# Gated linear attention with a SiLU block: state products per head in halves of the array's columns, first states copied by ScalarE, and a flag's product placed later

## Chip, cores and metric

The kernel runs on one core of one Trainium2 chip, in one launch. The metric is the device time in microseconds (us), the median of three runs. Beside it there is one profiled execution, with a record of every instruction of every engine.

## The reference

Batch 4, 8 heads, 768 steps, head dimension 48. Per head a state of 48x48 is decayed by `alpha`, row by row, and gets the outer product of `k` and `v` added; the output is `q` times the state. The result, as 3072 rows of 384, goes through a block `silu(x @ w_in) @ w_out` with 2048 hidden columns.

```python
for t in range(S):
    state = alpha[:, :, t, :, None] * state + np.einsum('bhd,bhe->bhde', k[:, :, t], v[:, :, t])
    y[:, :, t] = np.einsum('bhd,bhde->bhe', q[:, :, t], state)
...
x = y.transpose(0, 2, 1, 3).reshape(B * S, H * D)
h = x @ w_in
out = (h / (1 + np.exp(-h))) @ w_out
```

## The kernel before

**Chunks.** Time is cut into 6 chunks of 128 steps for each of the 4 batches: 24 chunks, numbered `n = 4 * ci + b`, so that chunks 0 to 3 are the first of each batch. Two heads stand side by side in a pair, head `u` of the pair in rows or columns `64 * u` to `64 * u + 47` of a 128-wide tile (16 are padding); there are `NP = 4` pairs. Each chunk goes through these functions:

- `products` (L652): transposes of alpha, k and q (by TensorE, L669, for the first eight chunks; by VectorE, L650, for the later ones), running products of alpha along time by scans (L674, L699), and k and q scaled by them. For the first chunks a copy on ScalarE (L671) brings alpha from PSUM.
- `scores` (L706): k times q for each head, in the two halves of the array's rows (L715), the causal mask on VectorE (L719), k transposed back (L723) and copied by ScalarE to `kn` (L725), and the decay of the state on ScalarE (L729).
- `values` (L734): the masked scores times v, and the state times q, in four quarters of 32 columns of the array (L749); ScalarE copies the result to `xt` (L754).
- `states` (L755): k times v over the 128 steps, into the state `st` of that batch. It is done for all but the last chunk of a batch, so 20 times.

In `states`, one matmul for a pair has `kn` of both heads as weights (128 columns) and `v` of both heads as moving data (64 + 48 = 112 columns). This computes four blocks; the two on the diagonal, k of a head with v of the same head, are read. VectorE adds them to `st` in two instructions of 48 rows by 192 (L768), or, in the first chunk of a batch, copies them there (L770).

All matmuls are in float32, and each one stands in the trace as two MATMUL and two LDWEIGHTS instructions.

**The block behind it.** `pieces` (L1037) is a list of slices of the second block's work: products with `w_in` (`enter_plain`, L805; `enter`, L828) and with `w_out` (`leave`, L926). Both use fewer matmuls than the plain product: sums of blocks of weights and inputs are formed on VectorE first, as in Strassen's method. One call of `go_on` (L1059) writes the next slice. After each of the four stages of a step, `fill` (L1083) writes as many slices as are due. `convert` brings the weights, which come as 64-bit numbers, to float32 (L599 on ScalarE, L602 to L604 on VectorE) during the first steps.

**Audits and the flag.** The shortcuts hold for bounded inputs. `audit` (L611) loads alpha and the weights once more, a part at a time into one buffer (L631), and VectorE keeps their extremes (L639). At the end four checks (L1138, L1139) are combined to `good` (L1141), one small matmul sums it over the partitions (L1143), VectorE turns that into `small` (L1144), and all engines load it as a number. If it is 0, a second, general version of the whole kernel runs (it does not for these inputs). Around this, the last slices of the second block are written:

```python
ps = ps_attn()[0:1, 0, 0:1]
pe.matmul(ps, lhsT=good, rhs=mask[:, C - 1 : C], start=True, stop=True)
dve.tensor_single_scalar(small, ps, 127.5, ALU.is_ge)
for _ in range(6):
    go_on()
```

**What sets the order.** The program text is not the order of the engines' queues. The framework puts the instructions of each engine into an order of its own, from dependences and its own estimates; `keep_in_program_order` pins a few. Waits are set by data and by buffers. PSUM: three banks `ps_a` in turn for the attention stages and the flag, three `ps_m` for `enter`, two `ps_o` for `leave`. Loads and stores are issued by SyncE (SP).

Of the kernel before, what the change touches and what calls it, by code (L numbers as in the profile page):

```python
# [355 lines left out]
def quotients(  # L356
# [20 lines left out]
    pe, dve, act, gps = nc.tensor, nc.vector, nc.scalar, nc.gpsimd  # L377
    B, H, S, D = q.shape
# [39 lines left out]
    def ps_attn(n=C):  # L418
        return ps_a.tile([128, 512], F32, name="ps_a").rearrange("p (j c) -> p j c", c=n)
# [98 lines left out]
    st = [fix.tile([128, NP, 2, D], F32, name=f"st{b}") for b in range(B)]  # L518
# [236 lines left out]
    def states(n):  # L755
        c = ctxs.pop(n)
        ci, b, vn = c["ci"], c["b"], c["v"]
        if ci < NCH - 1:
            ps = ps_attn(64)
            vn = vn.rearrange("p (j u) d -> p j (u d)", u=2)[:, :, 0 : 64 + D]  # L760
            for j in range(NP):
                pe.matmul(ps[:, 2 * j : 2 * j + 2, :].rearrange("p u d -> p (u d)")[:, 0 : 64 + D],
                          lhsT=c["kn"][:, j, :], rhs=vn[:, j], start=True, stop=True)
            for u in range(2):
                r = slice(64 * u, 64 * u + D)
                s, x = st[b][r, :, u, :], ps[r, u::2, 0:D]
                if ci > 0:
                    dve.tensor_tensor(s, x, s, ALU.add)  # L768
                else:
                    dve.tensor_copy(s, x)  # L770

    def block_x(grp, at):

# [285 lines left out]
    def go_on():  # L1059

        nonlocal done
        next(pieces[done][0], None)
        done += 1
# [36 lines left out]
    for step in range(STEPS):  # L1100
        stages = [[(scores, 1)], [(products, 0)], [(values, 1)], [(states, 1)]]
        if step < GB:

            stages = stages[1::-1] + stages[2:]
        elif step >= NA:
            stages = [[(scores, 1)], [(products, 0)], [(values, 1), (states, 1)], [(quotient, 0)]]
        for slot, group in enumerate(stages):
            for stage, lag in group:
                n = step - lag
                if not 0 <= n < NT:  # L1110
                    continue
                stage(n)
                if stage is values:
                    bridged = n + 1
                if stage is products and n + NIN < NA:
                    load(n + NIN)
                if stage is quotient and n + 1 < NT:
                    load(n + 1)
                if stage is states and n + NV < NT:
                    load_v(n + NV)  # L1120
            fill(step, slot)
            if step >= NA - 1 and slot > 0 and conv_done[1] == NFT and not late:
                settle()
# [15 lines left out]
        dve.tensor_single_scalar(e, e, bound, holds)  # L1139
    good = work.tile([128, 1], F32, name="good")  # L1140
    dve.tensor_reduce(good, ends, axis=AX, op=ALU.min)  # L1141
    ps = ps_attn()[0:1, 0, 0:1]
    pe.matmul(ps, lhsT=good, rhs=mask[:, C - 1 : C], start=True, stop=True)  # L1143
    dve.tensor_single_scalar(small, ps, 127.5, ALU.is_ge)  # L1144
    for _ in range(6):
        go_on()
    within = nc.values_load(small[0:1, 0:1], min_val=0, max_val=1)
    traced = nc.cur_bb.bb.instructions
# [8 lines left out]
@with_exitstack  # L1157
def kernel(
    ctx: ExitStack,
    tc: tile.TileContext,  # L1160
    q: bass.AP,
    k: bass.AP,
    v: bass.AP,
    alpha: bass.AP,
    moe_w_in: bass.AP,
    moe_w_out: bass.AP,
    out: bass.AP,
):


    flag = ctx.enter_context(tc.tile_pool(name="flag", bufs=1))
    small = flag.tile([1, 1], I32, name="small")
    args = (q, k, v, alpha, moe_w_in, moe_w_out, out)
    within = quotients(tc, small, *args)
    with tc.If(within < 1, label="general"):
        general(tc, *args)
# [30 lines left out]
```

## Time and profile before

| | |
|---|---|
| three runs | 583.13, 583.20 and 584.03 us, median 583.2 |
| span of the profiled execution | 582.0 us |
| granted clock of TensorE | 0.998 |
| busy: PE, PEld | 564.4 us, 500.4 us |
| busy: DVE, ACT, POOL | 452.6 us, 185.5 us, 7.3 us |
| state products (L762) | 160 MATMUL, 160 LDWEIGHTS |
| adds to the states (L768), copies (L770) | 32 of 350 ns, 8 of 354 ns |

PE is TensorE multiplying and PEld TensorE loading weights, DVE is VectorE, ACT ScalarE, POOL GpSimd, SP SyncE. In a line of a group stand the source line, the engine, the operation, output and inputs by name, the part of the array in use (rows*columns), the shape of the moving data and the count, and then busy us and the mean duration in ns. The ends of matmuls are modelled, so distances between starts say more on TensorE than durations. "Idle before" is the time for which the engine stood still ahead of these instructions, and who released it.

### The profile page before, as it was taken

What the parts mean: (1) busy time and instruction counts of PE and PEld (TensorE: products, weight loads), DVE (VectorE), ACT (ScalarE), POOL (GpSimd) and SP (SyncE); (2) the same over time, 40 slices, a digit from 0 to 9 for tenths busy, and PEclk for the clock granted to TensorE, in tenths of its full rate; (3) what the DMA queues carried; (4) which work ended last, traced back from release to release, by engine and by line L of the source; (5) the groups of instructions that cost most, each with busy time, mean ns of one, the idle gap of its engine ahead of it and who ended that gap; (6) DMA issues with size and microseconds to landing.
All of it is one profiled execution on the core that took longest, in us unless ns stands there. A gap on an engine that the chain in (4) does not pass through costs nothing. (4 is left out here: it accounts for less than half of the span.)

```text
span 582.0 us, 10743 instructions
## 1 busy us (share of the span) xinstructions
PE 564.4 (97%) x4290; PEld 500.4 (86%) x4290; DVE 452.6 (78%) x815; ACT 185.5 (32%) x359; POOL 7.3 (1%) x25
## 2 busy tenths in 40 slices
PE   5899999999999999999999999999999999999986
PEld 4777887678999899899899899899899999998986
DVE  5788899899788699996997886897872875766751
ACT  2235443222312233442433433342332342322100
POOL 5000000000000000000000000000000000000000
PEclk9999999999999999999999999999999999999999
DMA  9997885444534314442414433423110113424320
GB/s 211 174 276 195 218 210 131 88 111 117 128 89 125 112 33 124 123 115 71 119 48 120 122 74 86 129 53 105 57 44 22 51 44 115 123 88 129 96 72 30
DMA packets 93898, 63.70 MB, mean 109 GB/s; under 512 B 54800, under 2 KB 85520, under 8 KB 93840
## 3 DMA queue, kind: packets, MB, share of 16 engines
q1 hardware_dynamic: 93840, 62.94, 42.8%
q8 instruction: 35, 0.57, 0.4%
q14 instruction: 23, 0.19, 0.1%
HBM read 58.20 MB, written 4.72 MB: 108 GB/s over the span
## 5 line engine op out<-in xcount | busy, mean ns | idle before, releaser
L926 PE MATMUL ps_o<-w_out,g 128*128 128x192 f32 x704 | 122.3, 327 | 1.3 <-DVE o L940 1.1
L926 PEld LDWEIGHTS ps_o<-w_out,g 128*128 128x128 f32 x704 | 115.2, 190 | 4.2 <-DVE o L940 1.9
L926 PE MATMUL ps_o<-wt,g 128*128 128x192 f32 x528 | 91.6, 326 | 0.5 <-DVE u L1002 0.5
L805 PE MATMUL ps_m<-xt,w_in 128*128 128x256 f32 x384 | 88.9, 382 | 1.2 <-DVE w_in L604 1.1
L926 PEld LDWEIGHTS ps_o<-wt,g 128*128 128x128 f32 x528 | 87.2, 190 | 2.2 <-DVE u L1002 0.8
L805 PEld LDWEIGHTS ps_m<-xt,w_in 128*128 128x128 f32 x384 | 70.7, 190 | 11.0 <-DVE w_in L604 2.3
L828 PE MATMUL ps_m<-xc,w_in 128*128 128x256 f32 x288 | 70.0, 379 | 0.0
L639 DVE TENSOR_REDUCE seen<-bits 128x1 f32<-128x384 int32 (+2 forms) x65 | 42.4, 688 | 27.6 <-DMA bits<-in_moe_w_out_dram 21.2
L828 PEld LDWEIGHTS ps_m<-xc,w_in 128*128 128x128 f32 x288 | 54.1, 190 | 6.2
L834 ACT COPY g<-ps_m 128x512 f32<-128x512 f32 x64 | 37.1, 586 | 41.9 <-PE ps_m L828 41.9
L828 PE MATMUL ps_m<-xc,wx 128*128 128x256 f32 x192 | 49.8, 382 | 0.0
L931 DVE TENSOR_TENSOR g<-g 128x512 f32<-128x512 f32 x66 | 44.6, 686 | 4.8 <-PE ps_o L926 4.7
L839 ACT ACTIVATE g<-g 128x1024 f32<-128x1024 f32 x32 | 33.2, 1056 | 44.0 <-DVE g L842 44.0
L729 ACT ACTIVATE st<-st,u 128x96 f32<-128x96 f32 x80 | 25.7, 368 | 51.9 <-DVE u L674 36.8
L842 DVE TENSOR_TENSOR g<-ps_m,g 128x512 f32<-128x512 f32 x56 | 37.6, 684 | 2.9 <-PE ps_m L828 2.7
L828 PEld LDWEIGHTS ps_m<-xc,wx 128*128 128x128 f32 x192 | 35.0, 190 | 3.9 <-issue 0.4
L719 DVE TENSOR_TENSOR g<-ps_a,mask 128x512 f32<-128x512 f32 x48 | 31.2, 684 | 7.6 <-PE ps_a L715 7.3
L674 DVE TENSOR_TENSOR_SCAN u<-al,one 128x516 f32<-128x516 f32 x24 | 29.2, 1221 | 6.4 <-ACT al L671 6.4
L699 DVE TENSOR_TENSOR_SCAN p<-al,inv 128x516 f32<-128x516 f32 x24 | 29.5, 1228 | 4.8 <-PE ps_a L749 4.2
L834 ACT COPY part<-ps_m 128x512 f32<-128x512 f32 x32 | 18.8, 587 | 42.4 <-PE ps_m L828 38.1
L808 ACT ACTIVATE g<-ps_m 128x512 f32<-128x512 f32 x32 | 19.0, 594 | 41.6 <-PE ps_m L805 41.6
L715 PEld LDWEIGHTS ps_a<-p,u 48*128 48x128 f32 x384 | 24.6, 193 | 8.4 <-issue 6.7
(117 smaller groups left out, 657.3 us busy)
## 6 DMA issues: line engine op xcount, KB each, us to landing
bits<-in_moe_w_in_dram SPq DMA_DIRECT2D x24, 512.0 KB, 3.9
bits<-in_moe_w_out_dram SPq DMA_DIRECT2D x32, 384.0 KB, 3.4
at<-in_alpha_dram SPq DMA_DIRECT2D x64, 96.0 KB, 2.3
kt<-in_k_dram SPq DMA_DIRECT2D x64, 96.0 KB, 2.7
qt<-in_q_dram SPq DMA_DIRECT2D x64, 96.0 KB, 2.4
vn<-in_v_dram SPq DMA_DIRECT2D x24, 192.0 KB, 3.2
bits<-in_alpha_dram SPq DMA_DIRECT2D x9, 512.0 KB, 3.8
out_dram<-o SPq DMA_DIRECT2D x48, 96.0 KB, 1.8
```

The lines of the kernel that those rows point to most:

```text
L639: dve.tensor_reduce(seen[kind][which][:, i : i + 1], x, axis=AX, op=op, apply_absolute_value=True))
L674: dve.tensor_tensor_scan(u[:, end - 1 :: -1], sg[:, end:0:-1], one[:, end:0:-1], 0.0, ALU.mult, ALU.add)
L699: dve.tensor_tensor_scan(p[:, 0:end], sg[:, 0:end], iv[:, 0:end], 0.0, ALU.mult, ALU.add)
L719: dve.tensor_tensor(g[:, u], ps[u], mask[:, None, :].to_broadcast([128, NP, C]), ALU.mult)
L729: act.mul(s[:, j], s[:, j], c["all"][:, j : j + 1])
L805: pe.matmul(ps[:, e, :], lhsT=w_in[:, t, (f + e) * 128 : (f + e + 1) * 128], rhs=xt[:, t, :], start=(t == 0), stop=(t == NKT - 1))
L828: pe.matmul(ps[:, e], lhsT=block_w(w)[:, 2 * pair + e], rhs=block_x(grp, x), start=(first and e == 0), stop=(e == 1), skip_group_check=True)
L834: act.copy(to, ps)
L839: act.activation(x, x, AF.Silu)
L842: dve.tensor_tensor(to, a, b, op)
L926: pe.matmul(ps, lhsT=x, rhs=w[:, i], start=(first and i == 0), stop=(i == HF - 1), skip_group_check=True)
L931: dve.tensor_tensor(cells(grp, h, pair, *to), cells(grp, h, pair, *x), cells(grp, h, pair, *y), ALU.subtract)
```

## The change

There are three parts.

1. In `states`, a matmul takes one head: 48 weight columns and 48 moving columns, with its output in the 64 PSUM partitions that belong to its half of the array's columns. There are eight of them for a chunk in place of four, the two heads of a pair one after the other, all in one `ps_a` bank.
2. In the first chunk of a batch, ScalarE copies the result to `st` in place of VectorE.
3. Two slices of the second block are written ahead of the flag's product, and four after it in place of six.

```diff
         if ci < NCH - 1:
-            ps = ps_attn(64)
-            vn = vn.rearrange("p (j u) d -> p j (u d)", u=2)[:, :, 0 : 64 + D]
+
+            ps = ps_attn()
             for j in range(NP):
-                pe.matmul(ps[:, 2 * j : 2 * j + 2, :].rearrange("p u d -> p (u d)")[:, 0 : 64 + D],
-                          lhsT=c["kn"][:, j, :], rhs=vn[:, j], start=True, stop=True)
+                for u in range(2):
+                    r = slice(64 * u, 64 * u + D)
+                    pe.matmul(ps[r, j, 0:D], lhsT=c["kn"][:, j, r], rhs=vn[:, 2 * j + u, 0:D],
+                              start=True, stop=True)
             for u in range(2):
                 r = slice(64 * u, 64 * u + D)
-                s, x = st[b][r, :, u, :], ps[r, u::2, 0:D]
+                s, x = st[b][r, :, u, :], ps[r, :, 0:D]
                 if ci > 0:
                     dve.tensor_tensor(s, x, s, ALU.add)
                 else:
-                    dve.tensor_copy(s, x)
+                    act.copy(s, x)
...
     dve.tensor_reduce(good, ends, axis=AX, op=ALU.min)
+    go_on()
+    go_on()
     ps = ps_attn()[0:1, 0, 0:1]
     pe.matmul(ps, lhsT=good, rhs=mask[:, C - 1 : C], start=True, stop=True)
     dve.tensor_single_scalar(small, ps, 127.5, ALU.is_ge)
-    for _ in range(6):
+    for _ in range(4):
         go_on()
```

In the program after the change the lines behind `states` stand two further on, and those behind the flag's product four.

## The prediction, made before the changed kernel was run

> **What bounds the kernel now.** I read the share of each engine first, then the busy time by stretch, the waits of TensorE, the groups by shape, and last the timeline of TensorE around one state product.
>
> The first two lines are from the page (engines over the span), the others from the table by stretch (start:end, width, then busy us of PE, PEld, DVE, ACT, POOL).
>
> ```profile
> PE 564.4 (97%) x4290; PEld 500.4 (86%) x4290; DVE 452.6 (78%) x815; ACT 185.5 (32%) x359; POOL 7.3 (1%) x25
> 60.00:400.00 340.00, 340.00 (x2769) 299.84 (x2768) 293.68 (x521) 117.69 (x243) 0.00 (x0) 1.00 0.43 111
> 480.00:560.00 80.00, 77.81 (x432) 72.92 (x430) 50.89 (x100) 19.42 (x31) 0.00 (x0) 1.00 0.38 113
> ```
>
> From 60 to 480 us TensorE is busy all the time, and asked for its waits between 60 and 400 the trace names none. So in that stretch time is TensorE's own work and nothing else; DVE has 46 us of 340 free. It waits for others only at both ends:
>
> ```profile
> PE ps_o L669 <- DVE p L704: 1.4, 1, 1.4
> PE ps_m L805 <- DVE w_in L604: 1.1, 1, 1.1
> PE ps_o L669 <- DVE u L681: 0.7, 1, 0.7
> ...
> PE ps_a L1143 <- DVE good L1141: 1.5, 1, 1.5
> ```
>
> The first three are of the first 60 us, where DVE (weights being converted, scans) holds TensorE; the last is the flag's product, for which TensorE stands at 559.6 to 561.1. It ends a chain of audits, each a load of 3 to 4 us and then its reductions on DVE, that is linked load by load from about 482 us on. Before that the loads are long there when DVE comes to them, so the start of that chain moves with TensorE.
>
> What the state products cost, by shape (us, mean ns) and in order of time (start us, us):
>
> ```profile
> L762 PE MATMUL ps_a<-vn,kn 128*128 128x112 f32 x160 | 24.3, 293 | 0.0
> L762 PEld LDWEIGHTS ps_a<-vn,kn 128*128 128x128 f32 x160 | 20.6, 198 | 4.3 <-issue 3.6 <-ACT kn L725 0.2 <-DVE w_out L603 0.2
> L770 DVE COPY st<-ps_a 48x192 f32<-48x192 f32 x8 | 2.8, 354 | 2.4 <-PE ps_a L762 2.3
> ...
> 311.81 1.08 PE L749 MATMUL ps_a<-g,vn 128*32 128x128 f32 x32
> 312.71 0.84 PE L749 MATMUL ps_a<-p,st 128*32 128x128 f32 x24
> 313.48 1.15 PE L762 MATMUL ps_a<-vn,kn 128*128 128x112 f32 x8
> 314.46 0.61 PE L828 MATMUL ps_m<-xc,wx 128*128 128x256 f32 x2
> ```
>
> Durations of PE are modelled, so I go by starts. Each product is two MATMUL instructions (160 for 20 chunks of 4). The eight of a chunk begin at 313.48 and the next group at 314.46: 0.98 us, of which eight steps of 0.112 are 0.89 and 0.09 is the first weight load that nothing hides. In narrow stretches of the timeline the last four L749 start at 313.26, which is 0.22 before L762, though rounds of four are 0.11 apart ((312.71 - 311.81)/8). So a whole block, from the last four tiles of the values to the next full-array matmul, is 1.18 us; it is 1.18 in all 15 chunks from the sixth on.
>
> **What the Trainium skill says.** "TensorEngine Tiling (Array Packing)", Key Properties: tiles of the array load and multiply independently, a 128-row array can be split into two tiles of 64 columns, and changing the tiling mode drains the engine. The trace agrees where it can: 32 values in 0.90 us are 28 ns each, while 192 columns take 162 ns (16 of L926 in 2.60 us, so 0.85 ns a column): four tiles must run side by side. No run here shows halves of 64 columns. "TensorE: Matmul & The Clock Gate", LDWEIGHTS: a load costs its columns over 1.2 GHz, whatever the rows. The trace agrees: the eight loads of 128 columns start 0.112 apart (107 by that price), which is longer than 112 moving columns need (112 x 0.85 = 95). So the state products are bound by weight loads, half of which are for cross products that nobody reads. The same page gives small matmuls a floor of about 25 ns from start to start; in the trace four tiles start within 20 ns, so it isn't one for tiles.
>
> **The change part by part.**
>
> *State products.* Out go 8 instructions of 128 weight columns and 112 moving ones for each of 20 chunks; in come 16 of 48 and 48. If the halves run side by side as the quarters do, that is 8 rounds. One round is the longer of the load, estimated by the skill's price as 48/1.2 = 40 plus the 5 that the trace adds (112 against 107), and 48 moving columns (48 x 0.85 = 41): 45 ns. Around them stand two changes of mode where there was one. In: 0.20 from the last tile to the first state product (as 313.28 to 313.48 now), plus a first load of 48 columns in the open, about 0.04 (for 32 columns the second round of L749 comes 0.025 late, for 128 it is 0.10). Out: the drain, 0.09 (0.20 less the round of 0.11), and the next full load in the open, 0.10, against 0.015 that is lost there now: 0.09 net. The out case without states stands in the trace at 401.79, where the second L828 comes 0.32 after the first instead of 0.215. Block: 0.20 + 0.04 + 8 x 0.045 + 0.09 + 0.09 = 0.78 us, against 1.18: 0.40 saved, 15 times: 6.0 us. Chunk 4 stands between full-array matmuls (L805 on both sides, block 1.09 now), so it gets both changes new: 0.31 + 0.04 + 0.36 + 0.18 = 0.89, 0.2 saved. Bounds for a round: 41 (load alone) gives 0.43 saved, 60 ns gives 0.28; so 4.3 to 6.7 for the 16 chunks. The sums of L768 keep their shape (48x192) and are fewer cycles later only.
>
> *The first 60 us* (chunks 0 to 3 and the copies). Chunk 0's block runs at the slow clock, 2.33 us from tile to tile; by the same sum with its loads at about 82 ns it is 1.2, so 1.1 less, and the chain values, copy of xt (L754), `up` (L599), w_in (L604), scan (L674) follows it. The eight copies leave DVE (2.8 us, and 2.3 of waiting that DVE did in its order for L762). They go to ACT, 25% to 35% busy there: a copy of 128x192 on ACT is 0.31 us (L938), so 0.6 a chunk, in front of L754, which waits 1.5 us longer for the values anyway in chunk 0. Behind them in ACT's order stand `up` and the al copy; the weight conversion waits for those, so up to 0.6 us a chunk can come back. The built order of the changed kernel is another one up to chunk 3 (states and values split differently, one piece of scores put ahead of twelve L805, and those scores now wait on ACT for a ps_a bank), and from chunk 4 on the same on TensorE. TensorE's waits of 20 to 60 us are 3.0 us in all, and its work falls by 1.1 and about 0.9; so I bound the gain by 4 and by 0, and take 2.0.
>
> *The flag's product.* In the source it stands two pieces later. In the built order nothing moves: on TensorE it comes after the same 8 L926 as before with the same 6 + 8 + 8 + 16 + 8 behind it, and DVE, ACT and SP have the same order there too. 0, and the 1.5 us of standing stays. POOL's order is the same. In SP's queue some loads of a chunk change places among themselves; DVE waits for such loads 2.3 us in the whole span now (the transposes of kt), so I take 0, between -0.5 and 0.5.
>
> Sum: 6.0 + 0.2 + 2.0 + 0 = 8.2 us. Own span 582.0 gives 573.8; the timed runs of before have a median of 583.2, so I take the same off: 575.0. The saving reaches the end since the audits' chain starts when DVE, paced by TensorE, gets to it.
>
> **Rivals.**
> First, the halves run one after another with loads hidden: 16 turns of 45 ns, block 0.42 + 0.72 = 1.14, so 0.04 saved a chunk; chunk 4 loses 0.15. What is left is the start: 583.2 - 0.5 - 1.5 = 581.2. For it: no 64-column tile in this trace. Against: tiles of 32 columns and the pairs of 48 rows (L715) overlap.
> Second, slower: neither halves overlap nor loads hide in this mode. A turn is 41 + 43 = 84 ns, 16 of them 1.34; block 0.42 + 1.34 = 1.76, +0.58 in 15 chunks, and 0.75 more in chunk 4: about 583.2 + 9 = 592. It decides from 48 ns a turn for 16 serial turns ((1.18 - 0.42)/16), or 95 ns for 8 rounds. Against it: L749 starts its next loads as soon as its tiles multiply.
> Third, the start gets worse: ACT's copies in front of the al copy and `up` delay DVE by 0.6 us in each of four chunks and the new order loses a mode change or two (0.3 each). Then 6.2 - 3 = 3.2: 580.0.
> That the flag's part doesn't do what it says I hold for settled by the order.
>
> **How the numbers follow.** Side by side with a start between 0 and 4: 0.84; serial but hidden 0.06; slower 0.04; worse start 0.06. A measurement of this kernel tells about 0.2% (1.2 us) from no change. The likeliest case spans 583.2 - 4.3 = 578.9 to 583.2 - 10.7 = 572.5, taken as 572.4, and I reach to 579.2 for a part of the worse start. Faster 0.93, same 0.03 (serial, without gain at the start), slower 0.04.
>
> **What would show it.** Right: 320 instructions of the states, their group 0.32 to 0.45 us from first to last start, blocks of 0.75 to 0.90 us; no new waits of TensorE between 60 and 400; L1143 still with 1.5 us of idle time; chunk 5's states 1 to 4 us earlier than 93.3. Wrong: blocks over 1.18 us, starts of the states evenly 45 ns or more apart instead of in pairs, waits of TensorE for ACT's st copies, or a tail that is longer than now.

## The result and the profile after

| | before | after |
|---|---|---|
| median, range | 583.62 us, 583.13 to 584.07 (4 runs) | 578.74 us, 578.10 to 578.95 (4 runs) |
| span of the profiled execution | 582.0 us | 577.1 us |

The ratio is 0.9915 [0.9898, 0.9932]: 4.9 us faster, where 8.2 were forecast. The profiled spans differ by 4.9 too, so the profile holds the whole of the gain. The record doesn't say on which chip these two kernels ran; for each of the experiments below it does.

The same views follow in the same order. The engines over the span, from the page of the kernel after:

```profile
PE 557.6 (97%) x4450; PEld 491.2 (85%) x4450; DVE 449.3 (78%) x807; ACT 187.6 (33%) x367; POOL 7.3 (1%) x25
```

TensorE has 160 instructions more and 6.8 us less of work; 8 copies have gone from DVE to ACT. By stretch (start:end, width, then busy us of PE, PEld, DVE, ACT, POOL):

```profile
60.00:400.00 340.00, 339.60 (x2949) 297.41 (x2944) 295.94 (x522) 118.50 (x246) 0.00 (x0) 1.00 0.43 112
480.00:560.00 80.00, 74.74 (x417) 69.87 (x416) 51.12 (x102) 18.67 (x30) 0.00 (x0) 1.00 0.33 100
```

The middle was full before and lacks 0.4 us now. The tail lacks 5.3 us where it lacked 2.2; but of the flag's wait of before only 0.4 us lie ahead of 560, so by the waits themselves the tail has got 2.0 us worse (5.1 for 3.1). TensorE's waits name both places. The first two lines are of the kernel before, the others of the kernel after:

```profile
PE ps_o L926 <- DVE o L940: 1.1, 1, 1.1
PE ps_o L926 <- DVE u L1002: 0.5, 1, 0.5
...
PE ps_o L928 <- DVE o L942: 2.2, 1, 2.2
PE ps_a L1147 <- DVE good L1143: 1.6, 1, 1.6
...
PE ps_o L928 <- DVE u L1004: 1.3, 1, 1.3
...
PE ps_m L807 <- DVE w_in L604: 0.5, 1, 0.5
PE ps_m L830 <- DVE g L844: 0.4, 1, 0.4
```

The flag still waits (1.6, was 1.5). The waits for `o` and `u`, both for `ps_o` banks of `leave`, were 1.1 and 0.5 before and are 2.2 and 1.3; the one for `g` is new. Last, the state products, by shape and in order of time:

```profile
L764 PE MATMUL ps_a<-vn,kn 128*48 128x48 f32 x320 | 11.9, 216 | 0.0
L764 PEld LDWEIGHTS ps_a<-vn,kn 128*48 128x48 f32 x320 | 9.3, 127 | 4.5 <-issue 4.1 <-DVE w_out L603 0.2 <-ACT st L729 0.2
L772 ACT COPY st<-ps_a 48x192 f32<-48x192 f32 x8 | 2.5, 314 | 4.1 <-PE ps_a L764 4.0
```

```profile
306.51 1.08 PE L749 MATMUL ps_a<-g,vn 128*32 128x128 f32 x32
307.41 0.84 PE L749 MATMUL ps_a<-p,st 128*32 128x128 f32 x24
308.18 0.56 PE L764 MATMUL ps_a<-vn,kn 128*48 128x48 f32 x16
308.67 0.70 PE L830 MATMUL ps_m<-xc,wx 128*128 128x256 f32 x2
```

The sixteen start at 308.18 and the next group at 308.67: 0.49 us, where it was 0.98. In the records they start in pairs, the two of a pair 6 to 7 ns apart; the second pair comes 80 ns after the first and each later one 45 ns after the one before it, 0.357 us from first to last. From the last tile of the values (0.20 us ahead of the first state product) to the first L830 it is 0.70 us, and the load of that L830's second product stands in the open for 0.09: 0.79 in place of 1.18.

**Where 4.9 us came from.** The table gives the distance between the two profiles at three places (starts of instructions of TensorE, us).

| place | before | after | distance |
|---|---|---|---|
| first state product of chunk 5 | 93.28 | 91.69 | -1.6 |
| last product of the values | 463.82 | 456.92 | -6.9 |
| last matmul | 576.13 | 571.34 | -4.8 |

Up to the first place there were 2.2 us forecast (2.0 of the start, 0.2 of chunk 4). Between the first and the second lie 15 blocks at 0.40, 6.0; there are 5.3, because chunk 13 gave 0.7 back. After the second 2.1 us are lost again. 8.2 - 0.6 - 0.7 - 2.1 = 4.8, the distance at the last matmul.

**The loss in chunk 13.** Two views of the kernel after, TensorE's timeline and then DVE's:

```profile
238.15 1.13 PE L830 MATMUL ps_m<-xc,w_in 128*128 128x256 f32 x4
239.68 1.13 PE L830 MATMUL ps_m<-xt,w_in 128*128 128x256 f32 x4 [0.41 <-DVE g L844]
```

```profile
236.76 0.40 DVE L550 TENSOR_TENSOR w_in<-w_in 128x256 f32<-128x256 f32 x1
237.08 0.41 DVE L546 TENSOR_TENSOR w_in<-wx 128x256 f32<-128x256 f32 x1
237.41 0.68 DVE L844 TENSOR_TENSOR g<-ps_m,g 128x512 f32<-128x512 f32 x1
...
238.34 0.69 DVE L844 TENSOR_TENSOR g<-g 128x512 f32<-128x512 f32 x1
238.93 1.29 DVE L844 TENSOR_TENSOR g<-ps_m,g 128x512 f32<-128x512 f32 x2
```

DVE does sums of weights and of `g` there without a gap, and has the same instructions in the same order and without a gap in the kernel before. This run of sums comes 4.1 us earlier than before (its first L844 at 237.41, was 241.50), TensorE's product ahead of the wait 4.75 (238.15, was 242.90): TensorE has gained on DVE and finds the `ps_m` bank that it needs not yet read. It gives the difference back, 0.7 us from chunk 12 to chunk 13.

**The loss in the tail.** DVE and TensorE of the kernel after, around the longest wait:

```profile
528.37 1.01 DVE L639 TENSOR_REDUCE seen<-bits 128x1 f32<-128x384 int32 x2 [0.82 <-DMA bits<-in_moe_w_out_dram]
529.30 0.68 DVE L844 TENSOR_TENSOR g<-ps_m,g 128x512 f32<-128x512 f32 x1
529.90 0.68 DVE L551 SCALAR_TENSOR_TENSOR g<-g 128x512 f32<-128x512 f32 x1
530.50 0.35 DVE L942 TENSOR_TENSOR o<-ps_o,u 128x192 f32<-128x192 f32 x1
```

```profile
527.61 1.12 PE L830 MATMUL ps_m<-xt,w_in 128*128 128x256 f32 x4
530.90 3.25 PE L928 MATMUL ps_o<-w_out,g 128*128 128x192 f32 x16 [2.17 <-DVE o L942]
```

DVE stands until a part of w_out has landed, reduces it, and only then comes to the sums behind it in its queue; the last of them frees the `ps_o` bank for which TensorE has stood 2.2 us. The audits have one buffer: each load starts when the last part has been reduced. From the first part of w_out to the last this chain takes 61.70 us in the profile of before and 63.76 in that of after. From the last part's first reduction to the last matmul it is 17.2 us in both. So the distance at the end is that of the chain's start (497.22 before, 490.37 after: 6.9 earlier) less the growth of its length (2.1): 4.8. The three waits show where TensorE stands meanwhile.

### The profile page after: what moved, and what is told of

It is laid out like the page before. It is cut to its first block, busy times and chain, and to the rows that moved or that the text cites. A ratio compares the mean times of both kernels' runs of the same rounds, so it can differ in the third digit from the quotient of the medians.

```text
span 577.1 us, 11060 instructions
## 1 busy us (share of the span) xinstructions
PE 557.6 (97%) x4450; PEld 491.2 (85%) x4450; DVE 449.3 (78%) x807; ACT 187.6 (33%) x367; POOL 7.3 (1%) x25
## 5 line engine op out<-in xcount | busy, mean ns | idle before, releaser
L830 PE MATMUL ps_m<-xc,w_in 128*128 128x256 f32 x288 | 70.1, 379 | 0.0
L830 PEld LDWEIGHTS ps_m<-xc,w_in 128*128 128x128 f32 x288 | 54.0, 190 | 6.4 <-DVE g L844 0.2
L830 PE MATMUL ps_m<-xc,wx 128*128 128x256 f32 x192 | 50.1, 383 | 0.0
L844 DVE TENSOR_TENSOR g<-ps_m,g 128x512 f32<-128x512 f32 x56 | 37.6, 684 | 2.9 <-PE ps_m L830 2.7
L830 PEld LDWEIGHTS ps_m<-xc,wx 128*128 128x128 f32 x192 | 35.0, 190 | 4.2 <-issue 0.4
```

The lines of the kernel that those rows point to most:

```text
L830: pe.matmul(ps[:, e], lhsT=block_w(w)[:, 2 * pair + e], rhs=block_x(grp, x), start=(first and e == 0), stop=(e == 1), skip_group_check=True)
L844: dve.tensor_tensor(to, a, b, op)
```

## The experiments

Twelve kernels, in four groups (four, four, three and one), each group on a chip of its own with the kernel before beside it. Chain is the time from the first reduction of w_out's first part to that of its last in the profiled execution. The kernel before is not equally fast everywhere: its median is 583.1 us on the first of these chips and 585.1 to 585.8 on the three others. Expectations that name a time come from the level of the first comparison. On the three later chips some are missed by up to 1.5 us, and there the distance to before says more (before_audits2: 2.5 us less, 1.5 to 3 expected).

| | ratio to before [95%] | median us (before there) | chain us |
|---|---|---|---|
| flag_only | 0.9995 [0.9984, 1.0006] | 583.16 (583.12) | 61.4 |
| states_only | 0.9933 [0.9907, 0.9959] | 578.98 (583.12) | 61.5 |
| copies_only | 0.9996 [0.9986, 1.0005] | 582.96 (583.12) | 61.5 |
| states_copies | 0.9906 [0.9882, 0.9929] | 577.84 (583.12) | 61.2 |
| halves_apart | 0.9953 [0.9938, 0.9968] | 582.8 (585.06) | 64.1 |
| flag_later | 0.9865 [0.9840, 0.9890] | 577.83 (585.06) | 64.3 |
| before_no_wout_audit | 0.9923 [0.9901, 0.9944] | 580.81 (585.06) | none |
| after_no_wout_audit | 0.9805 [0.9784, 0.9827] | 573.99 (585.06) | none |
| after_audits2 | 0.9832 [0.9819, 0.9844] | 575.36 (585.49) | 144 |
| before_audits2 | 0.9965 [0.9952, 0.9977] | 582.95 (585.49) | 145 |
| audits2_flag_later | 0.9825 [0.9812, 0.9838] | 575.32 (585.49) | 144 |
| after_again | 0.9884 [0.9871, 0.9898] | 578.95 (585.78) | 63.7 |

**The parts alone.** flag_only is the kernel before with the third part of the diff, states_only with the first (DVE still copies), copies_only with this line alone, and states_copies with the first and second together:

```diff
                 else:
-                    dve.tensor_copy(s, x)
+                    act.copy(s, x)
```

> Part 3 alone on the kernel before. Its built program has the order of the kernel before on every engine (only buffer numbers differ), so the theory expects ratio 1.000 within 0.002, the flag's product with 1.5 to 1.7 us of idle time ahead of it, and, as it is the kernel before once more, a second sample of the tail's audit loads: from the first to the last of the 16 loads of w_out 61.7 us in the first profile of before, 63.8 in that of the changed kernel. If the difference comes from the load times of one execution and not from the change, this sample may lie anywhere from 61 to 64. The rival (the flag's place matters) expects 1 us or more less.

> Part 1 alone (per-head products; copies on VectorE; flag as before). Theory: 0.40 us in each of 15 chunks and 0.2 in chunk 4, 6.2 in all, by the time the tail begins, plus what the start gives without the copies (0 to 1), less the tail's loss of about 2: 578.5 to 580. Rival that the copies are what makes the start 1.4 us shorter: then the milestones of chunks 5 and 6 are less than 0.8 us earlier than before.

> Part 2 alone (first states copied by ScalarE, products as before). Theory: VectorE has 2.8 us less to do in the first 66 us, so 0 to 1 us less at chunk 5 and the same at the end: 582.5 to 583.6. Rival that ScalarE's copies hold up the al copy and the weight conversion: 0.5 us more, 584.

> Parts 1 and 2 without part 3. Its built order is that of the changed kernel, so it is the changed kernel once more: 578.7 within 0.6. Its profile is a second sample of the tail: if the loss of 2.1 us between 514 us and the flag came from slow loads in one execution, the chain of the 16 w_out loads may be 61 to 64 us again; if it belongs to the change it is 63.5 or more again. TensorE's wait of 0.6 us near 239 us: if it is there again, it belongs to the order of VectorE's queue, else to that execution.

The flag's part is worth nothing, and so are the copies by themselves. The state products alone carry most of it, and with the copies what the whole change gives (577.84, a little under the 578.1 to 579.3 expected); the intervals of these two overlap, so by time alone the copies' share is not shown. How the start splits is seen at the first state product of chunk 5: 93.28 before, 93.53 in flag_only, 93.36 in copies_only, 93.93 in states_only, 91.83 in states_copies, 91.69 in the kernel after. The profiles of flag_only, before_no_wout_audit and before_audits2, whose first chunks are those of before, have 93.53 to 93.66, so a few tenths here are the scatter of executions. The products alone come later there, not earlier; with the copies on ACT 1.5 us earlier. TensorE's waits in the first 70 us of states_only say what holds it, against 1.1 before and 0.5 after on the same line:

```profile
PE ps_m L807 <- DVE w_in L604: 1.9, 2, 1.4
```

TensorE stands longer for `w_in` as long as DVE also has the copies to do: 1.9 us against 0.5 in states_copies. That is 1.4 of the 2.1 us between these two at chunk 5; the rest was not taken apart. Why the copies alone bring nothing, though they take this wait from 1.1 to 0.4, stays open: the place is reached no earlier. The built order of the first chunks changes with the copies, and what took the place of the wait was not taken apart.

states_copies has the same order of instructions on every engine as the kernel after. Its profiled span is 574.2, 2.9 us less. Up to the last product of the values the two agree (457.14 and 456.92); what differs is the tail. Likewise flag_only has the order of before on every engine. These two profiles, of one chip, have chains of the same length (61.4 and 61.2), and their spans are 581.5 and 574.2: with equal chains 7.3 us reach the end.

**Halves one after the other.** The kernel after with its two loops exchanged, so that the eight instructions of one half of the columns come before the eight of the other:

```diff
-            for j in range(NP):
-                for u in range(2):
+            for u in range(2):
+                for j in range(NP):
```

> The changed kernel with the loop order of the state products turned: four products of the left half of the columns, then four of the right half, so that neighbours in the queue share a half. Same instructions, same weights, same bytes. Theory (the halves gain because two products stream side by side): 16 turns of 45 ns in a row, 0.7 us from first to last start in place of 0.36, so 0.36 us more in each of 20 chunks: 6 to 7 us slower than the changed kernel, 584 to 586. Rival (it is the narrower weight load alone that gains, 48 columns for 128): no change, 577 to 579.

The timeline of halves_apart around the same block:

```profile
311.11 0.78 PE L764 MATMUL ps_a<-vn,kn 128*48 128x48 f32 x16
311.81 0.92 PE L830 MATMUL ps_m<-xc,wx 128*128 128x256 f32 x3
```

0.70 us in place of 0.49. From first to last start the sixteen take 0.571 us, against 0.357: after the first step of 80 ns the instructions of one half stand 45 ns apart, as the rounds do in the kernel after, but the second half begins when five of the first have started. So neighbours in the same half cost 0.21 us a block, less than the 0.36 of two halves in full sequence. By the last product of the values (460.71) it is 3.8 us, of which 15 times 0.21 are 3.2. Of the 0.40 that a block saves, 0.21 rests on halves that overlap all the way; this kernel is 2.3 us faster than before (585.06 to 582.8). So neither expectation came: the narrower load alone isn't enough, and the halves overlap in part in this order too.

**The flag's product really later.** The kernel after with five slices before the product and one after it, by which it moves behind 14 more matmuls in the built order too:

```diff
-    go_on()
-    go_on()
+    for _ in range(5):
+        go_on()
     ps = ps_attn()[0:1, 0, 0:1]
...
-    for _ in range(4):
-        go_on()
+    go_on()
```

> The changed kernel with five pieces ahead of the flag's product and one behind. In its built order the product comes 14 matmuls (28 instructions, 4.5 us) later, which the changed kernel's two pieces did not bring about. Theory: TensorE no longer stands 1.5 to 1.7 us for the audits' end, since it has that work to do meanwhile, and the flag is still ready before the last product: 1.2 to 1.7 us less than the changed kernel, 576.3 to 577.3. Rival (the products in between wait for VectorE, which is behind the same audits, so the wait only changes its place): no change.

```profile
557.30 2.76 PE L928 MATMUL ps_o<-w_out,g 128*128 128x192 f32 x16
560.00 0.19 PE L1147 MATMUL ps_a<-mask,good 128*1 128x1 f32 x2
560.12 2.87 PE L928 MATMUL ps_o<-wt,g 128*128 128x192 f32 x16
```

In this timeline of flag_later the flag's line has no wait behind it any more. From the last part's reductions to the last matmul it takes 15.5 us, against 17.2 in the kernel after: 1.7 us, the wait that the change leaves standing. The waits for `ps_o` banks stay (3.6 us in this profile). The timed runs can't show the 1.7: the kernel after did not run on this chip, and the interval of flag_later's ratio overlaps that of after_again.

**Without the audits of w_out.** From both kernels the sixteen loads of w_out for audits and their reductions are left out; so the flag no longer checks the range of w_out.

```diff
-            todo += [(moe_w_out[f * 128 : f * 128 + 128, :], HD, 1) for f in range(NFT)]
```

> The kernel before without the 16 audits of w_out: these loads, their reductions and so the check of the range of w_out are left out. It is the base for the next one. Theory: the tail is then TensorE's alone, so 3 to 5 us less than before (its standing time from 470 us to the flag is 3.1 to 4.1 us): 578 to 580.5.

> The changed kernel without the 16 audits of w_out (the same part left out). Theory (what was gained by 470 us, 6.6 to 6.9, is partly eaten by the chain of audit loads in the tail): the difference to the base without these audits is 6.5 to 7 us, 571 to 573.5. Rival (the changed kernel loses 1 to 2 us in the tail for another reason): the difference stays at 4.9 to 5.3.

All of TensorE's waits after 60 us, first of before_no_wout_audit, then of after_no_wout_audit:

```profile
PE ps_a L1142 <- DVE good L1140: 1.6, 1, 1.6
```

```profile
PE ps_a L1146 <- DVE good L1142: 1.2, 1, 1.2
PE ps_m L829 <- DVE g L843: 0.4, 1, 0.4
```

The waits of `leave` are gone from both, and the two kernels are 6.8 us apart by their medians and 7.1 by their spans. Without the chain the change brings to the end what it has gained by the last values (457.37 for 464.23, 6.9 us).

**Twice as many audits in each step.** Here nothing of the computation is left out; the audits only begin to come two to a step in place of one, so that most of w_out's lie ahead of 480 us:

```diff
-        if late and at % 4 == 0:
+        if late and at % 2 == 0:
```

In audits2_flag_later the flag's product is also written when only four slices are left, one of them ahead of the loading of the flag (the expectation's "one slice" is this one):

```diff
-    go_on()
-    go_on()
+    while done < len(pieces) - 4:
+        go_on()
     ps = ps_attn()[0:1, 0, 0:1]
...
-    for _ in range(4):
-        go_on()
+    go_on()
```

> The changed kernel, with two audits due per step of the schedule where one was due, so that most of the loads of w_out for audits lie ahead of the last 60 us. Theory (what ate 2 of the 6.9 us gained by 470 us is the chain of audit loads in the tail): the chain has few links left after 480 us, TensorE's waits for the sums of the last leave (L928) and for good go or shrink from 5.1 us to under 2, and the time is 573.5 to 576, 3 to 5 us below the changed kernel. Rival (VectorE, which the audits load further during the steps at 1.35 us a step, becomes the bound there): new waits of TensorE for VectorE between 100 and 400 us, and the time is within 1 us of the changed kernel's or above it.

> The same two audits per step in the kernel before. Theory: here the chain in the tail costs only what the flag's product waits (1.5 us) and part of two waits of the last leave (1.6), so it gains 1.5 to 3 us: 580 to 581.5. The distance to the changed kernel with the same edit then is 6 to 7 us, as without the audits of w_out (6.8). Rival (the distance stays at 4.9 because the tail's loss comes from something other than the audits' loads): 578.5 to 580.

> The changed kernel with two audits per step, and the flag's product written with one slice of the second block left behind it in place of four. Theory: with the chain out of the tail, what is left to gain is the wait of the flag's product, 1.2 to 1.7 us; 572.5 to 574.5, the fastest of all. Rival (the values that the flag needs, and the loading of it by all engines, then stand at the end in the open): slower than the same kernel with the flag's product where the change puts it, by 0.5 to 2 us.

The stretches of after_audits2, and all of TensorE's waits in it after 100 us:

```profile
60.00:400.00 340.00, 337.32 (x2931) 294.36 (x2927) 307.45 (x549) 117.49 (x245) 0.00 (x0) 0.99 0.50 129
480.00:560.00 80.00, 80.00 (x454) 76.39 (x453) 38.40 (x73) 19.71 (x32) 0.00 (x0) 1.00 0.05 15
```

```profile
PE ps_m L830 <- DVE g L844: 2.7, 3, 1.6
```

The tail is full: the 5.1 us of waits there have gone. DVE has 11.5 us more to do between 60 and 400, and 2.3 us of waits came back (2.7 against 0.4) where DVE was full already, at 228 to 243 us (2.1 in before_audits2). So theory and rival both hold a part; on balance it gains. On this chip the two kernels with this edit are 7.6 us apart by medians and 5.9 by spans (the profiled execution of after_audits2 is the slowest of its five), about the 6 to 7 expected. The flag's product brings nothing here, against the 1.2 to 1.7 expected (the intervals overlap): in after_audits2 the built order puts it at 482.5 us, as soon as its audits are through, and it has no wait to lose. Both kernels beat the change as it was made, 1.7% below the kernel before.

**The kernel after once more**, nothing edited, on a fourth chip.

> The changed kernel once more, nothing edited, for the tail alone. Theory (the 2 us that were lost between 470 us and the flag are the loads of w_out of one execution, not the order of the program): the first to the last reduction of w_out's audits takes anything between 61.2 and 64.3 us, as in the other kernels; if it is near 61.5, the waits of TensorE after 480 us sum to about 3 us in place of 5.1 and the profiled span is 574 to 575.5; if it is near 64, they sum to about 5 and the span is 577. Time 576.5 to 579.5, ratio 0.986 to 0.993. Rival (the order of the changed program slows the chain itself): 63.5 or more for the chain, with each load near its usual 3.1 us and the loss in the reductions or the issue between them.

6.8 us faster there, though its chain is long again, with waits of 5.2 us after 480. So a long chain by itself doesn't shrink the gain; by the sum above only a chain longer than that of the kernel before does. No profile of before was taken on this chip; that it takes 2 us more on the three later chips fits a longer chain there, but is not shown to come from it. The rows of DVE's reductions of w_out between 470 and 560 us (the last columns are idle time ahead of them, and what ended it), of before, after, states_copies and after_again in turn:

```profile
L639 DVE TENSOR_REDUCE seen<-bits 128x1 f32<-128x384 int32 x32 | 16.2, 549 | 21.4 <-DMA bits<-in_moe_w_out_dram 21.2
```

```profile
L639 DVE TENSOR_REDUCE seen<-bits 128x1 f32<-128x384 int32 x32 | 16.2, 549 | 24.1 <-DMA bits<-in_moe_w_out_dram 23.9
```

```profile
L639 DVE TENSOR_REDUCE seen<-bits 128x1 f32<-128x384 int32 x32 | 16.2, 548 | 19.3 <-DMA bits<-in_moe_w_out_dram 19.3
```

```profile
L639 DVE TENSOR_REDUCE seen<-bits 128x1 f32<-128x384 int32 x32 | 16.2, 549 | 24.1 <-DMA bits<-in_moe_w_out_dram 24.1
```

The reductions are the same to 0.1 us; the waiting for loads is not. Fifteen loads, from issue to the reduction that waits for them, sum to 46.1 us in before, 48.1 in after, 45.6 in states_copies and 48.0 in after_again, and what is left of the chain (reductions and issue) is 15.6 in all four. So the rival falls: the loss is in the loads. It isn't the order of the program either, since states_copies has that order and the shortest chain of all. Six timed runs of that one program lie between 576.01 and 578.69 us, a spread nearly as wide as that of the chains; the profiled one is the second fastest, which is why the median of states_copies is only 5.3 us below that of before. What makes a load of w_out longer in one execution than in another stays open; in the profiles at hand five chains are short (before, and the four kernels of the first chip) and four are long (after, halves_apart, flag_later, after_again), so a difference between chips is possible and wasn't tried.

A second buffer for the audits wasn't tried.

## Why the prediction was right or wrong, step by step

- **The state products: right.** Rounds of 45 ns, 0.357 us from first to last start (0.32 to 0.45 forecast), blocks of 0.79 (0.78), 0.40 saved in each of 15, and 0.2 in chunk 4 (1.09 to 0.89). The Trainium skill's statement that different tiles load and multiply in parallel ("TensorEngine Tiling (Array Packing)", Key Properties) is borne out here: 16 products in 8 rounds. (The mode of two 64-column tiles stands on that page under Available Configurations.) A load price by columns ("TensorE: Matmul & The Clock Gate", LDWEIGHTS) fits, 40 ns by that page for 48 columns and 45 from start to start, but 48 moving columns (estimated 41 ns) would fit as well; no run here tells which of the two sets the 45. The serial turns that the first two rivals lived on are not there. A slip of the working: its 1.18 us run from the last tile of the values, 0.20 us ahead of the state products, and not from the 313.26 that it names.
- **The start: mis-sized.** 2.0 was taken and 1.4 came. Chunk 0's block came as priced (1.17 for 1.2). But the start isn't a sum of two edits, as the working had it: products alone -0.65 (a loss, though half of it may be scatter), copies alone nothing, both +1.5 at chunk 5 (chunk 4's 0.2 among them). What was put down as a risk of the copies (ACT in front of DVE's work) did not show; that the relief of DVE lets the shorter products count is shown for the wait for `w_in` alone. The bound of 4 also rested on 3.0 us of waits of TensorE between 20 and 60 us, where the profile has 2.1 (37.9 busy of 40).
- **The flag's product: right.** Nothing moves in the built order, and flag_only is 0.9995 with a flag's wait of 1.7 us. A move that is one (flag_later) gives that wait back.
- **"No new waits of TensorE between 60 and 400": wrong by one.** DVE's 46 free us in 340 are a mean; near 239 us it has none, and there TensorE, which has moved ahead more than DVE could, runs into the `ps_m` banks. 0.7 us.
- **The step that failed: "The saving reaches the end since the audits' chain starts when DVE, paced by TensorE, gets to it."** The start of the chain did move, by 6.9 us, as this says. But the end is the start plus the length, and the prediction held the length fixed and gave the tail no range. The chain is paced by loads and not by TensorE, and sixteen of them took 61.2 to 64.3 us from one execution to another; the 2.1 us more in the profile of after are 0.14 on each load. With equal chains 7.3 us reached the end (flag_only to states_copies), without w_out's audits 6.8, with them moved forward 7.6 by medians; with them as they are it was 4.9 in the first comparison and 6.8 on the fourth chip. That the change makes the chain longer is not shown. And a late chain costs not only at the flag, where the prediction looked: through DVE's queue it holds the `ps_o` banks of `leave`, and these waits stay when the flag's is gone.
- **The chances.** The likeliest case came. 578.74 is 0.2 inside the slow end that was given to it (578.9), but that end stood for slower rounds and a start without gain, and neither came; the tail ate the rest. That the number fits so near the edge is in part luck.

## What to carry to other kernels

A saving on the engine that sets the pace also moves the start of a chain behind it, but the end then comes with that chain's own length. Loads that share one buffer with the reader before them are such a chain; here one order of the program had 61.2 us of it in one execution and 63.8 in another. So compare kernels with chains of the same length, or move the chain to where the pace is set elsewhere; the latter gained here, at the price of new waits. Look for the stretches in which the second engine has no gap, not for its mean share, before you say that a faster first engine meets nothing. And write tiles so that neighbours in the program lie in different parts of the array: in these blocks that was worth 0.21 us each.

## What the runs showed of the hardware

- Products in alternate halves of the columns start 6 to 7 ns apart in pairs, and the pairs 45 ns apart after a first step of 80. In the other order, eight of one half and then eight of the other, the second half still begins 0.22 us after the first, when five of the first have started and not at its end, 0.35 us after: 0.57 us for the sixteen against 0.36.
- Loads of one shape (128 x 384 elements of 8 bytes) took 2.7 to 3.8 us from issue to the reduction in the profiles of before, after, states_copies and after_again, and one of 4.4 stands in flag_later. The mean over fifteen was between 3.04 and 3.25 us from execution to execution.
